# Retention attention by chunks of 128 tokens with carried sums, two head pairs at a time

## The chip, the cores and the metric

The kernel runs on one core of one Trainium2 chip. The metric is device time in microseconds: the median of a few runs of the whole launch.

## The reference

Eight batches of eight heads, 576 tokens and head size 64 go through a retention layer: scores are weighted by a power of gamma that depends on the distance, with no softmax. Its output, read as 4608 tokens of 512 features, goes through an MLP of width 2048 with a PReLU. Everything is fp32 (the MLP weights arrive as float64 bits).

```python
scores = (1.0 / np.sqrt(D)) * np.matmul(q, k.transpose(0, 1, 3, 2))
gamma = 1.0 - 2.0 ** (-5.0 - np.arange(H))
rel = pos[:, None] - pos[None, :]
Dmat = np.where(rel >= 0, gamma[:, None, None] ** rel[None], 0.0)
attn = np.matmul(scores * Dmat, v)                  # (B, H, S, D)
x = attn.transpose(0, 2, 1, 3).reshape(B * S, H * D)
h = x @ w_in
g = np.maximum(h, 0.0) + alpha * np.minimum(h, 0.0)
out = g @ w_out
```

## The kernel before

Heads are taken in pairs: 32 pairs (batch b, pair c), and two heads of 64 fill the 128 partitions. `load_pair` issues nine DMAs for a pair on SyncE's queue, two pairs ahead of use (three buffers). `transposes` turns Q and K to have the head dimension on partitions, ten 128-column TensorE transposes into PSUM tiles of the pool `ps_a`; ScalarE scales and copies Q out, VectorE copies K out. `scores` makes, for each of the five chunks of keys, the scores of all later queries (1600 columns for each head), in four groups that each fill a PSUM bank for each head; VectorE multiplies every piece by a table `decay` on its way to SBUF (line 245). `values` multiplies by V, 1600 columns for each head again, and ScalarE copies the result into x^T. The two heads of a pair use different halves of the TensorE array: different rows in the scores, different columns in the value products. A full fp32 matmul is two TensorE passes in the trace, each with a load of its stationary operand; a transpose is one.

The MLP runs in units of one block of 384 tokens and one chunk of 128 of the 2048 hidden features, 12 x 16 = 192 units: four products into `ph` (line 192), two VectorE operations for the PReLU (lines 196 and 198), three products into `po` (line 177). At the end of a block ScalarE copies `po` out and GpSimd's queue issues the stores (lines 183, 185).

The weights come in 32 pieces of 128 x 512 during the first two batches, four pieces for each pair. GpSimd issues the DMA of a piece (line 142); two GpSimd operations (149, 150), five on VectorE (151 to 161) and one more on GpSimd (163) round float64 bits to fp32. Two buffers hold raw pieces. The pieces alternate, four of `w_in` and four of `w_out`, so that each eight pieces make four more units of any block runnable.

The framework orders the instructions of each engine ahead of time from the order of the program, by its own estimates of readiness; at run time every engine executes its list in that order, and semaphores do the rest. Attention of batch b + 1 is written between MLP units of the batches up to b; batches 0 and 1 have no units written among them, but the framework may move units up. x^T is held in tiles of two batches, two buffers. `ps_a` has three buffers of one bank, `ph` two, `po` three.

Of the kernel before, what the change touches and what calls it, by code (L numbers as in the profile page):

```python
# [18 lines left out]
def kernel(  # L19
# [10 lines left out]
    nc = tc.nc  # L30
# [5 lines left out]
    NPAIR = H // 2              # head pairs in a batch; pair c fills rows c*128.. of x^T  # L36
    NCH = (S + P - 1) // P      # key chunks
    NFULL = S // P
    REM = S - NFULL * P
    msz = [min(P, S - P * i) for i in range(NCH)]  # L40
    NCC = DM // P
    NFC = DFF // P
    GB = 2                      # batches in one x^T tile
    TB = 384                    # tokens in an MLP block
    NTC = TB // P
    NKB = NTOK // TB
    SH = S // 2                 # queries in one pass of the value product
    WQ = 4                      # pieces in which the weights are loaded

    assert D == 64 and 2 * D == P and DM == H * D and NTOK == B * S  # L50
    assert (GB * S) % TB == 0 and B % GB == 0 and SH <= 512 and 0 < REM
    assert NPAIR == NCC and DM <= 512 and NFC % WQ == 0

    # Columns of chunk t in the transposed weights: queries P*t .. S.
    atoff = [sum(S - P * j for j in range(i)) for i in range(NCH)]
    ATW = sum(S - P * j for j in range(NCH))
    # Score groups, one PSUM bank each: (chunk, first query, last query, column in the bank)
    groups = [[(0, 0, 512, 0)],
              [(0, 512, S, 0), (1, P, S, S - 512)],
              [(2, 2 * P, S, 0), (3, 3 * P, S, S - 2 * P)],  # L60
              [(4, 4 * P, S, 0)]]
    assert S == 576 and NCH == 5
# [5 lines left out]
    nat = ctx.enter_context(tc.tile_pool(name="nat", bufs=3))  # L68
# [5 lines left out]

    pairs = [(b, c) for b in range(B) for c in range(NPAIR)]

    def load_pair(b, c):
        tiles = []
        for name, src in (("q", q), ("k", k), ("v", v)):
            t = nat.tile([P, NCH, 2, D], FP32, tag=f"nat_{name}", name=f"{name}n_{b}_{c}")  # L80
            for h2 in range(2):
                nc.sync.dma_start(
                    t[:, 0:NFULL, h2, :],
                    src[b, 2 * c + h2, 0:NFULL * P, :].rearrange("(j p) d -> p j d", p=P))
            nc.sync.dma_start(
                t[0:REM, NFULL, :, :],
                src[b, 2 * c:2 * c + 2, NFULL * P:S, :].rearrange("h p d -> p h d"))
            tiles.append(t)
        return tiles

    loaded = {0: load_pair(*pairs[0]), 1: load_pair(*pairs[1])}
# [4 lines left out]
    # decay[p, h, w] = gamma_h ** (w - p) for w >= p, otherwise 0.  The chunk t of  # L96
    # keys sees query s at w = s - P*t, so that one table serves all chunks.
    rel = const.tile([P, S], FP32, name="rel")
    nc.gpsimd.iota(rel, pattern=[[1, S]], base=0, channel_multiplier=-1,
                   allow_small_or_imprecise_dtypes=True)  # L100
    nc.gpsimd.affine_select(out=rel, in_=rel, compare_op=ALU.is_ge, fill=1.0e8,
                            base=0, pattern=[[1, S]], channel_multiplier=-1)
    decay = const.tile([P, H, S], FP32, name="decay")
    for h in range(H):
        nc.scalar.activation(decay[:, h, :], rel, ACTF.Exp,
                             scale=float(np.log1p(-(2.0 ** (-5.0 - h)))))
# [25 lines left out]
    # High words as fp32 patterns, which order as the doubles do: the largest whose  # L132
    # exponent fp32 has, and the smallest.
# [3 lines left out]
    def load_weights(n):  # L137
        for _ in range(min(n, len(pieces))):
# [9 lines left out]
            # Saturate above fp32's range, zero below it.  # L148
# [4 lines left out]
            # Sign and top exponent bit stay, the rest moves up by three: the double  # L153
            # cut to the 20 bits of mantissa in its high word.
# [4 lines left out]
            # The low word counts 2^-52 of the signed power of two.  # L159
# [8 lines left out]
    pend = []       # (block, chunk, activations) whose output products are still to come  # L168
# [42 lines left out]
    def transposes(qn, kn, b, c):  # L211
        qk = []
        for name, src in (("q", qn), ("k", kn)):
            dst = attn.tile([P, S], FP32, tag=f"{name}T", name=f"{name}T_{b}_{c}")
            for j0, j1 in ((0, 3), (3, NCH)):
                c0, c1 = j0 * P, min(j1 * P, S)
                pt = ps_a.tile([P, 512], FP32, tag="psa", name=f"pt{name}_{b}_{c}_{j0}")
                for j in range(j0, j1):
                    nc.tensor.transpose(  # L219
                        pt[:, j * P - c0:j * P - c0 + msz[j]],  # L220
                        src[0:msz[j], j, :, :].rearrange("p h d -> p (h d)"),
                        ident[0:msz[j], 0:msz[j]])
                if name == "q":
                    nc.scalar.mul(dst[:, c0:c1], pt[:, 0:c1 - c0], 1.0 / float(np.sqrt(D)))  # L224
                else:
                    nc.vector.tensor_copy(dst[:, c0:c1], pt[:, 0:c1 - c0])  # L226
            qk.append(dst)
        return qk

    def scores(qT, kT, b, c):  # L230
        at = [attn.tile([P, ATW], FP32, tag=f"at{h2}", name=f"at{h2}_{b}_{c}")
              for h2 in range(2)]
        for gi, grp in enumerate(groups):
            ps = [ps_a.tile([P, 512], FP32, tag="psa", name=f"ps{h2}_{b}_{c}_{gi}")
                  for h2 in range(2)]
            for t, s0, s1, co in grp:
                for h2 in range(2):
                    nc.tensor.matmul(ps[h2][0:msz[t], co:co + s1 - s0],  # L238
                                     kT[h2 * D:(h2 + 1) * D, P * t:P * t + msz[t]],
                                     qT[h2 * D:(h2 + 1) * D, s0:s1],  # L240
                                     start=True, stop=True)
            for h2 in range(2):
                for t, s0, s1, co in grp:
                    w0, w1 = s0 - P * t, s1 - P * t
                    nc.vector.tensor_tensor(  # L245
                        out=at[h2][0:msz[t], atoff[t] + w0:atoff[t] + w1],
                        in0=ps[h2][0:msz[t], co:co + s1 - s0],
                        in1=decay[0:msz[t], 2 * c + h2, w0:w1],
                        op=ALU.mult)
        return at  # L250

    def values(vn, at, b, c):
        grp, x0 = b // GB, (b % GB) * S
        for s0 in range(0, S, SH):
            s1 = s0 + SH
            po = ps_a.tile([P, 512], FP32, tag="psa", name=f"pv_{b}_{c}_{s0}")
            chunks = [t for t in range(NCH) if P * t < s1]
            for t in chunks:
                lo = max(s0, P * t)
                a0 = atoff[t] - P * t  # L260
                for h2 in range(2):
                    nc.tensor.matmul(po[h2 * D:(h2 + 1) * D, lo - s0:s1 - s0],  # L262
                                     vn[0:msz[t], t, h2, :],
                                     at[h2][0:msz[t], a0 + lo:a0 + s1],
                                     start=(t == chunks[0]), stop=(t == chunks[-1]))
            nc.scalar.copy(xT[grp][:, c, x0 + s0:x0 + s1], po[:, 0:SH])  # L266

    # Block kb of the MLP can start when the batch of its last token is done.
# [7 lines left out]
    WB = 2                                      # batches over which the weights arrive  # L276
    WPP = -(-len(pieces) // (WB * NPAIR))

    prev = None
    for i, (b, c) in enumerate(pairs):  # L280
        if c == 0 and b % GB == 0:
            xT[b // GB] = xpool.tile([P, NCC, GB * S], FP32, tag="xT", name=f"xT_{b // GB}")
        if i + 2 < len(pairs):
            loaded[i + 2] = load_pair(*pairs[i + 2])
        qn, kn, vn = loaded.pop(i)
        qT, kT = transposes(qn, kn, b, c)
        if prev is not None:
            values(*prev)
        if c == 0 and b > 0:
            enqueue(b - 1)  # L290
        share = -(-len(queue) // (NPAIR - c)) if b >= WB else 0
        pop_units(share // 2)
        at = scores(qT, kT, b, c)
        if b < WB:
            load_weights(WPP)
        pop_units(share - share // 2)
        prev = (vn, at, b, c)
    values(*prev)
    enqueue(B - 1)
    pop_units(len(queue))  # L300
    while pend:
# [31 lines left out]
```

## Time and profile before

| | us |
|---|---|
| median of 3 runs | 1415.12 (1414.74 to 1418.02) |
| span of the profiled execution | 1413.1 |
| TensorE busy with matmuls | 1343.5 |
| VectorE busy | 494.1 |
| GpSimd busy | 136.8 |
| ScalarE busy | 75.7 |

The span runs from the first to the last instruction of one execution that the hardware profiler recorded; that execution has no time of its own beside it, and the median of the runs lies 2.0 us above the span. Busy times of an engine are unions. TensorE's weight loads are counted apart (PEld) and overlap its matmuls (PE).

### The profile page before, as it was taken

How to read it: one execution, taken by the hardware profiler on the slowest of the kernel's cores; microseconds unless marked ns; L12 is line 12 of the kernel's file. 1: busy time of each engine (PE TensorE's matmuls, PEld its weight loads, DVE VectorE, ACT ScalarE, POOL GpSimd, SP SyncE). 2: the span in 40 equal slices, each digit the busy share in tenths (PEclk: the TensorE clock that was granted, in tenths of full speed). 3: DMA queues.
4: the chain of work that ended last, by engine and by line, in shares of the span. 5: the costliest groups of instructions: out<-in, count | busy, mean ns of one | idle time of the engine just before them, and what ended most of it. 6: DMA issues, size and time to landing. Idle time of an engine off the chain costs nothing.

```text
span 1413.1 us, 11632 instructions
## 1 busy us (share of the span) xinstructions
PE 1343.5 (95%) x4801; PEld 704.8 (50%) x4801; DVE 494.1 (35%) x993; ACT 75.7 (5%) x173; POOL 136.8 (10%) x173
## 2 busy tenths in 40 slices
PE   6878989999999999999999999999999999999997
PEld 3434444555545555554555555555555555555553
DVE  4677765323232333223223323332233232322221
ACT  2000000000000000000000100000000000000000
POOL 4544453000000000000000000000000000000000
PEclk9668789999999999999999999999999999999999
DMA  7434432010101111110110111101101100000000
GB/s 192 109 108 119 116 92 61 23 26 0 48 1 33 40 26 26 48 26 0 48 26 0 51 40 33 48 0 26 48 0 26 48 9 1 0 23 0 23 0 23
DMA packets 122773, 55.30 MB, mean 39 GB/s; under 512 B 116304, under 2 KB 116320, under 8 KB 122720
## 3 DMA queue, kind: packets, MB, share of 16 engines
q1 hardware_dynamic: 115200, 28.33, 9.0%
q0 software_dynamic: 7520, 26.23, 5.6%
q8 instruction: 38, 0.62, 0.2%
q14 instruction: 15, 0.12, 0.0%
HBM read 45.10 MB, written 9.44 MB: 39 GB/s over the span
## 4 chain that ended last, share of the span: by engine, by line
issue 44%; PE 40%; DMA 7%; POOL 5%; DVE 4%; SPq 0%; POOLq 0%; ACT 0%; ACTq 0%; DVEq 0%
PE ph L192 16%; PE po L177 16%; PE ps L238 4%; DMA raw<-in_moe_w_in_dram 3%; DMA raw<-in_moe_w_out_dram 3%; PE pv L262 3%; POOL wb L150 2%; DVE at L245 1%; POOL wa L149 1%; POOL w_in L163 1%; POOL w_out L163 1%; PE ptk L219 1%; POOL out_dram L185 1%; DVE wa L151 1%; PE ptq L219 1%
## 5 line engine op out<-in xcount | busy, mean ns | idle before, releaser
L192 PE MATMUL ph<-xT,w_in 128*128 128x384 f32 x1536 | 549.7, 495 | 0.0
L177 PE MATMUL po<-w_out,g 128*128 128x512 f32 x1152 | 536.7, 601 | 0.2 <-POOL wa L149 0.2
L192 PEld LDWEIGHTS ph<-xT,w_in 128*128 128x128 f32 x1536 | 285.1, 191 | 215.3 <-issue 73.3
L196 DVE TENSOR_SCALAR neg<-ph,alpha 128x384 f32<-128x384 f32 x192 | 118.5, 617 | 691.7 <-PE ph L192 691.7
L177 PEld LDWEIGHTS po<-w_out,g 128*128 128x128 f32 x1152 | 219.5, 192 | 233.4 <-issue 182.8
L238 PE MATMUL ps<-qT,kT 64*128 64x64 f32 (+5 forms) x768 | 167.5, 449 | 45.9 <-DVE at L245 43.2
L245 DVE TENSOR_TENSOR at<-ps,decay 128x192 f32<-128x192 f32 (+5 forms) x384 | 146.5, 426 | 88.9 <-PE ps L238 85.9
L238 PEld LDWEIGHTS ps<-qT,kT 64*128 64x128 f32 (+1 forms) x768 | 93.5, 189 | 154.5 <-DVE at L245 90.8
L185 POOL DMA_DIRECT2D out_dram<-osb x36 | 19.5, 542 | 1152.4 <-ACT osb L183 1152.4
L262 PE MATMUL pv<-at,vn 128*64 128x288 f32 (+4 forms) x1024 | 108.1, 359 | 3.3 <-DVE kT L226 2.8
L198 DVE SCALAR_TENSOR_TENSOR g<-ph,neg 128x384 f32<-128x384 f32 x192 | 106.9, 557 | 6.2
L262 PEld LDWEIGHTS pv<-at,vn 128*64 128x64 f32 (+1 forms) x1024 | 65.5, 144 | 45.9 <-issue 14.9
L224 ACT ACTIVATE qT<-ptq 128x384 f32<-128x384 f32 x64 | 23.3, 408 | 916.7 <-PE ptq L219 916.7
L226 DVE COPY kT<-ptk 128x384 f32<-128x384 f32 x64 | 29.0, 455 | 70.1 <-PE ptk L219 70.1
L151 DVE SCALAR_TENSOR_TENSOR wa<-wb,wa 128x512 f32<-128x512 f32 x32 | 36.1, 1128 | 44.6 <-POOL wb L150 44.5
L219 PE MATMUL ptk<-ident,kn 128*128 128x128 f32 (+1 forms) x160 | 34.2, 304 | 4.0 <-DMA kn<-in_k_dram 3.3
L183 ACT COPY osb<-po 128x512 f32<-128x512 f32 x36 | 21.1, 585 | 258.7 <-PE po L177 258.7
L150 POOL TENSOR_TENSOR wb<-wa 128x512 f32<-128x512 f32 x32 | 34.1, 1067 | 2.1
L266 ACT COPY xT<-pv 128x288 f32<-128x288 f32 x64 | 25.5, 399 | 153.4 <-PE pv L262 153.4
L219 PEld LDWEIGHTS ptq<-ident,qn 128*128 128x128 f32 (+1 forms) x160 | 21.6, 150 | 24.3 <-issue 19.2
L219 PE MATMUL ptq<-ident,qn 128*128 128x128 f32 (+1 forms) x160 | 29.2, 296 | 3.4 <-DVE at L245 3.4
L219 PEld LDWEIGHTS ptk<-ident,kn 128*128 128x128 f32 (+1 forms) x160 | 20.2, 150 | 21.4 <-issue 14.5
(23 smaller groups left out, 166.4 us busy)
## 6 DMA issues: line engine op xcount, KB each, us to landing
out_dram<-osb POOLq DMA_DIRECT2D x36, 256.0 KB, 2.4
qn<-in_q_dram SPq DMA_DIRECT2D x64, 128.0 KB, 2.5
kn<-in_k_dram SPq DMA_DIRECT2D x64, 128.0 KB, 2.8
raw<-in_moe_w_in_dram POOLq DMA_DIRECT2D x16, 512.0 KB, 4.3
vn<-in_v_dram SPq DMA_DIRECT2D x64, 128.0 KB, 2.6
raw<-in_moe_w_out_dram POOLq DMA_DIRECT2D x16, 512.0 KB, 3.7
qn<-in_q_dram SPq DMA_DIRECT2D x32, 32.0 KB, 2.6
kn<-in_k_dram SPq DMA_DIRECT2D x32, 32.0 KB, 2.5
```

The costliest lines, as they stand in the source:

```text
L150: nc.gpsimd.tensor_tensor(out=b, in0=a, in1=a, op=ALU.mult)
L151: nc.vector.scalar_tensor_tensor(out=a, in0=b, scalar=HI_MIN * HI_MIN, in1=a, op0=ALU.is_ge, op1=ALU.mult)
L177: nc.tensor.matmul(acc[kb][m], g[:, m * P:(m + 1) * P], w_out[fc // FCQ][:, fc % FCQ, :], start=(fc == 0), stop=(fc == NFC - 1))
L185: nc.gpsimd.dma_start(out[t0:t0 + P, :], osb)
L192: nc.tensor.matmul(ph, w_in[fc // FCQ][:, cc, f0:f0 + P], xT[grp][:, cc, t0:t0 + TB], start=(cc == 0), stop=(cc == NCC - 1))
L196: nc.vector.tensor_scalar(neg, ph, 0.0, alpha[:, fc:fc + 1], ALU.min, ALU.mult)
L198: nc.vector.scalar_tensor_tensor(out=g, in0=ph, scalar=0.0, in1=neg, op0=ALU.max, op1=ALU.add)
L219: nc.tensor.transpose(pt[:, j * P - c0:j * P - c0 + msz[j]], src[0:msz[j], j, :, :].rearrange("p h d -> p (h d)"), ident[0:msz[j], 0:msz[j]])
L226: nc.vector.tensor_copy(dst[:, c0:c1], pt[:, 0:c1 - c0])
L238: nc.tensor.matmul(ps[h2][0:msz[t], co:co + s1 - s0], kT[h2 * D:(h2 + 1) * D, P * t:P * t + msz[t]], qT[h2 * D:(h2 + 1) * D, s0:s1], start ...
L245: nc.vector.tensor_tensor(out=at[h2][0:msz[t], atoff[t] + w0:atoff[t] + w1], in0=ps[h2][0:msz[t], co:co + s1 - s0], in1=decay[0:msz[t], 2 ...
L262: nc.tensor.matmul(po[h2 * D:(h2 + 1) * D, lo - s0:s1 - s0], vn[0:msz[t], t, h2, :], at[h2][0:msz[t], a0 + lo:a0 + s1], start=(t == chunks ...
```

## The change

Attention is computed chunk by chunk. For a chunk j of 128 queries, the keys of the same chunk are handled by masked scores as before, but all earlier keys come in through a running sum of k^T v, a 64 x 64 matrix for each head, that is added up over the chunks. The decay is split into a factor on the query (`qtab`) and one on the key (`ktab`, `krem`), so that the scores need only a causal 0/1 mask. Sequences of 576 give four whole chunks and 64 tokens that are left; the rests of two head pairs are put side by side as one chunk of 128, with a block mask `maskr`.

Two pairs (a couple, four heads) are worked on together: 16 couples. Loads are 18 DMAs for each couple, buffers for two couples. GpSimd multiplies K by its factor in place, five operations for each couple. Each couple has 18 transposes, of which VectorE takes Q out with its factor and ScalarE takes K out. `scores` makes 18 products of 128 columns and masks them in six VectorE operations. `states`, new, makes 16 products of 64 columns and adds them up in eight VectorE operations of 64 partitions, into block-diagonal 128 x 128 matrices `sums` (two sets). `values` makes 18 products of 128 columns within the chunks and then eight full-width products of the sums with Q. The setup has some eighty small memsets and small tables in place of the 128 x 8 x 576 table. Values of a couple now come in the same step as its scores, with MLP units in three places, and the weights come in eight pieces for each couple. The MLP and the weight conversion are unchanged.

```diff
-    nat = ctx.enter_context(tc.tile_pool(name="nat", bufs=3))
+    nat = ctx.enter_context(tc.tile_pool(name="nat", bufs=2))
...
+    def load_couple(b, u):
+        tiles = []
+        for name, src in (("q", q), ("k", k), ("v", v)):
+            t = nat.tile([P, NJ, 4, D], FP32, tag=f"nat_{name}", name=f"{name}n_{b}_{u}")
+            r = nat.tile([P, 2, D], FP32, tag=f"rem_{name}", name=f"{name}r_{b}_{u}")
+            for j in range(NJ):
+                nc.sync.dma_start(
+                    t[:, j, :, :],
+                    src[b, 4 * u:4 * u + 4, j * C:(j + 1) * C, :].rearrange("h p d -> p h d"))
+            for i in range(2):
+                h = 4 * u + 2 * i
+                nc.sync.dma_start(
+                    r[i * REM:(i + 1) * REM, :, :],
+                    src[b, h:h + 2, NJ * C:S, :].rearrange("h p d -> p h d"))
+            tiles += [t, r]
+        return tiles
...
+    for j in range(NJ):
+        for h in range(H):
+            nc.gpsimd.memset(ktab[:, j, h:h + 1], float(np.exp(lng[h] * (MID - j * C))))
...
+            for j in range(NJ + 1):
+                nc.gpsimd.memset(qfac[rows, c, j:j + 1],
+                                 float(np.exp(lng[2 * c + h2] * (j * C - MID)) / np.sqrt(D)))
...
+    for i in range(2):
+        s_ = const.tile([P, NJ, 2, P], FP32, name=f"sums{i}")
+        nc.gpsimd.memset(s_, 0.0)
...
+    def transposes(n, b, u, tiles):
+        qn, qr, kn, kr, vn, vr = tiles
+        nc.gpsimd.tensor_tensor(
+            out=kr, in0=kr, in1=krem[:, u, :, None].to_broadcast([P, 2, D]), op=ALU.mult)
+        for j in range(NJ):
+            nc.gpsimd.tensor_tensor(
+                out=kn[:, j], in0=kn[:, j],
+                in1=ktab[:, j, 4 * u:4 * u + 4, None].to_broadcast([P, 4, D]), op=ALU.mult)
...
+        for i in range(2):
+            pt = ps_a.tile([P, NJ * C], FP32, tag="psa", name=f"ptq{i}_{n}")
+            for j in range(NJ):
+                nc.tensor.transpose(
+                    pt[:, j * C:(j + 1) * C],
+                    qn[:, j, 2 * i:2 * i + 2, :].rearrange("p h d -> p (h d)"), ident)
+            nc.vector.tensor_tensor(out=qT[i], in0=pt, in1=qtab[:, 2 * u + i, 0:NJ * C],
+                                    op=ALU.mult)
...
+            nc.scalar.copy(kT[i], pt)
+        return qT, kT, rT
+
+    def scores(n, qT, kT, rT):
+        at = []
+        for i in range(2):
+            ps = [ps_a.tile([P, NJ * C], FP32, tag="psa", name=f"ps{i}{h2}_{n}")
                   for h2 in range(2)]
+            for j in range(NJ):
                 for h2 in range(2):
+                    rows, cols = slice(h2 * D, (h2 + 1) * D), slice(j * C, (j + 1) * C)
+                    nc.tensor.matmul(ps[h2][:, cols], kT[i][rows, cols], qT[i][rows, cols],
+                                     start=True, stop=True)
             for h2 in range(2):
+                a = attn.tile([P, NJ, C], FP32, tag=f"at{i}{h2}", bufs=1, name=f"at{i}{h2}_{n}")
+                nc.vector.tensor_tensor(
+                    out=a, in0=ps[h2].rearrange("p (j w) -> p j w", w=C),
+                    in1=mask[:, None, :].to_broadcast([P, NJ, C]), op=ALU.mult)
+                at.append(a)
...
+    def states(n, tiles):
+        qn, qr, kn, kr, vn, vr = tiles
+        ps = ps_a.tile([P, NJ, 2, D], FP32, tag="psa", name=f"pu_{n}")
+        for j in range(NJ):
+            for i in range(2):
+                for h2 in range(2):
+                    nc.tensor.matmul(ps[h2 * D:(h2 + 1) * D, j, i, :], kn[:, j, 2 * i + h2, :],
+                                     vn[:, j, 2 * i + h2, :], start=(j == 0 and i == 0),
+                                     stop=(j == NJ - 1 and i == 1), skip_group_check=True)
+        sm = sums[n % 2]
+        for j in range(NJ):
+            for h2 in range(2):
+                hd = slice(h2 * D, (h2 + 1) * D)
+                if j == 0:
+                    nc.vector.tensor_copy(sm[hd, 0, :, hd], ps[hd, 0, :, :])
+                else:
+                    nc.vector.tensor_tensor(out=sm[hd, j, :, hd], in0=ps[hd, j, :, :],
+                                            in1=sm[hd, j - 1, :, hd], op=ALU.add)
+
+    def values(n, b, u, tiles, qT, rT, at):
...
+        for i in range(2):
+            for j in range(NJ):
                 for h2 in range(2):
+                    nc.tensor.matmul(pv[i][h2 * D:(h2 + 1) * D, j * C:(j + 1) * C],
+                                     vn[:, j, 2 * i + h2, :], at[2 * i + h2][:, j, :],
+                                     start=(j == 0), stop=False, skip_group_check=True)
...
+        for i in range(2):
+            for j in range(1, NJ):
+                nc.tensor.matmul(pv[i][:, j * C:(j + 1) * C], sm[:, j - 1, i, :],
+                                 qT[i][:, j * C:(j + 1) * C],
+                                 start=False, stop=(j == NJ - 1), skip_group_check=True)
+            nc.scalar.copy(xT[grp][:, 2 * u + i, x0:x0 + NJ * C], pv[i])
...
+    for n, (b, u) in enumerate(couples):
...
+        share = -(-len(queue) // (NC2 - u)) if b >= WB else 0
+        qT, kT, rT = transposes(n, b, u, tiles)
+        pop_units(share // 3)
+        at = scores(n, qT, kT, rT)
+        states(n, tiles)
         if b < WB:
+            load_weights(WPC)
+        pop_units(share // 3)
+        values(n, b, u, tiles, qT, rT, at)
+        pop_units(share - 2 * (share // 3))
+        if u == NC2 - 1:
+            enqueue(b)
```

## Rows read from the trace of the kernel before

**Rows 1.** The page's slices: TensorE's busy share in 40 equal slices, in tenths.

```profile
PE   6878989999999999999999999999999999999997
```

**Rows 2.** Line 163, last step of a weight piece: count, duration min/median/max, first and last start.

```profile
L163 POOL TENSOR_TENSOR w_out<-wa,wb x16: 1250/1260/1649, 46.0 to 233.4; 128x512 f32<-128x512 f32 x16
```

**Rows 3.** Windows, 0 to 234.7 us: busy time and count by engine, granted clock, DMA.

```profile
0.00:234.70 234.70, 194.34 (x753) 101.12 (x755) 159.91 (x313) 20.27 (x46) 117.30 (x137) 0.82 0.45 118
```

**Rows 4.** Chain of waits, 95 to 130 us: start, length, what.

```profile
99.05 3.55 DMA raw<-in_moe_w_out_dram
...
102.76 0.66 POOL wa L149
...
103.49 1.03 POOL wb L150
104.53 1.18 POOL w_out L163
105.70 3.74 DMA raw<-in_moe_w_out_dram
```

**Rows 5.** Windows, 234.7 to 1405.2 us, of lines 192, 177, 238 and 262 in turn.

```profile
234.70:1405.20 1170.50, 507.89 (x1438) 265.72 (x1438) 1.00 0.09 23
...
234.70:1405.20 1170.50, 495.40 (x1086) 206.34 (x1086) 1.00 0.09 23
...
234.70:1405.20 1170.50, 104.83 (x552) 60.09 (x552) 1.00 0.09 23
...
234.70:1405.20 1170.50, 74.03 (x756) 45.36 (x752) 1.00 0.09 23
```

**Rows 6.** Timeline of TensorE, 1303 to 1316 us: start, length, instructions.

```profile
1304.45 2.74 PE L192 MATMUL ph<-xT,w_in 128*128 128x384 f32 x8
...
1309.61 2.74 PE L192 MATMUL ph<-xT,w_in 128*128 128x384 f32 x8
```

**Rows 7.** Chain of waits, 670 to 790 us: one head pair among MLP units.

```profile
677.00 0.65 PE ph L192 x2
677.96 3.06 PE pv L262 x32
...
701.19 1.11 PE ps L238 x4
...
706.28 0.84 PE ph L192 x2
707.38 2.13 PE ph L192 x6
...
729.63 3.07 PE pv L262 x32
```

**Rows 8.** Timeline of TensorE, 1399 to 1406 us: the last products.

```profile
1399.82 5.31 PE L177 MATMUL po<-w_out,g 128*128 128x512 f32 x12
```

**Rows 9.** Timeline, 675 to 683 us: the transposes of Q and their loads.

```profile
675.72 0.80 PE L219 MATMUL ptq<-ident,qn 128*128 128x128 f32 x5
675.72 0.36 PEld L219 LDWEIGHTS ptq<-ident,qn 128*128 128x128 f32 x3 [0.29 <-issue]
```

**Rows 10.** Groups by line and shape, VectorE, line 245: busy us, mean ns, idle before.

```profile
L245 DVE TENSOR_TENSOR at<-ps,decay 128x512 f32<-128x512 f32 x64 | 41.9, 685 | 61.9 <-PE ps L238 61.9
...
L245 DVE TENSOR_TENSOR at<-ps,decay 128x192 f32<-128x192 f32 x64 | 22.1, 346 | 0.0
...
L245 DVE TENSOR_TENSOR at<-ps,decay 128x64 f32<-128x64 f32 x64 | 13.9, 218 | 13.2 <-PE ps L238 13.2
```

**Rows 11.** Timeline, 0 to 40 us: two small memsets of GpSimd.

```profile
0.31 0.10 POOL L317 MEMSET const-bfloat16-1.0<- 128x1 bf16 x1
0.35 0.10 POOL L317 MEMSET const-uint8-127<- 128x1 uint8 x1
```

**Rows 12.** Groups by line and shape: TensorE's weight loads of lines 238 and 262.

```profile
L238 PEld LDWEIGHTS ps<-qT,kT 64*128 64x128 f32 x640 | 80.2, 198 | 114.2 <-DVE at L245 60.1 <-issue 34.5 <-PE po L177 3.0
L262 PEld LDWEIGHTS pv<-at,vn 128*64 128x64 f32 x896 | 59.3, 145 | 37.0 <-issue 6.0 <-DVE kT L226 3.0 <-DVE wa L160 0.8
```

More of the change, by code (lines that the diff above doesn't have):

```diff
@@ L36 @@
     NPAIR = H // 2
[L37 to L40, printed above, removed]
+    NC2 = NPAIR // 2
+    C = P
+    NJ = S // C
+    REM = S - NJ * C
+    MID = S // 2
     NCC = DM // P
@@ L46 @@
     NKB = NTOK // TB
-    SH = S // 2
     WQ = 4
     assert D == 64 and 2 * D == P and DM == H * D and NTOK == B * S
[L51 to L62, printed above, removed]
+    assert (GB * S) % TB == 0 and B % GB == 0 and 2 * REM == P and NJ == 4
+    assert NPAIR == NCC and DM <= 512 and NFC % WQ == 0 and NC2 == 2
     const = ctx.enter_context(tc.tile_pool(name="const", bufs=1))
@@ L73 @@
     ps_o = ctx.enter_context(tc.tile_pool(name="ps_o", bufs=NTC, space=bass.MemoryType.PSUM))
-    pairs = [(b, c) for b in range(B) for c in range(NPAIR)]
-    def load_pair(b, c):
+    couples = [(b, u) for b in range(B) for u in range(NC2)]
+    def load_couple(b, u):
         tiles = []
         for name, src in (("q", q), ("k", k), ("v", v)):
-            t = nat.tile([P, NCH, 2, D], FP32, tag=f"nat_{name}", name=f"{name}n_{b}_{c}")
-            for h2 in range(2):
+            t = nat.tile([P, NJ, 4, D], FP32, tag=f"nat_{name}", name=f"{name}n_{b}_{u}")
+            r = nat.tile([P, 2, D], FP32, tag=f"rem_{name}", name=f"{name}r_{b}_{u}")
+            for j in range(NJ):
@@ L89, in load_pair @@
+            tiles += [t, r]
         return tiles
-    loaded = {0: load_pair(*pairs[0]), 1: load_pair(*pairs[1])}
+    loaded = {0: load_couple(*couples[0]), 1: load_couple(*couples[1])}
     ident = const.tile([P, P], FP32, name="ident")
     make_identity(nc, ident)
-    rel = const.tile([P, S], FP32, name="rel")
-    nc.gpsimd.iota(rel, pattern=[[1, S]], base=0, channel_multiplier=-1,
+    lng = [float(np.log1p(-(2.0 ** (-5.0 - h)))) for h in range(H)]
+    wrow = const.tile([P, C], FP32, name="wrow")
@@ L100 @@
+    nc.gpsimd.iota(wrow, pattern=[[1, C]], base=0, channel_multiplier=0,
                    allow_small_or_imprecise_dtypes=True)
-    nc.gpsimd.affine_select(out=rel, in_=rel, compare_op=ALU.is_ge, fill=1.0e8,
-                            base=0, pattern=[[1, S]], channel_multiplier=-1)
-    decay = const.tile([P, H, S], FP32, name="decay")
-    for h in range(H):
-        nc.scalar.activation(decay[:, h, :], rel, ACTF.Exp,
-                             scale=float(np.log1p(-(2.0 ** (-5.0 - h)))))
+    prow = const.tile([P, 1], FP32, name="prow")
@@ new lines @@
+    nc.gpsimd.iota(prow, pattern=[[1, 1]], base=0, channel_multiplier=1,
+                   allow_small_or_imprecise_dtypes=True)
+    mask = const.tile([P, C], FP32, name="mask")
+    nc.gpsimd.memset(mask, 1.0)
+    nc.gpsimd.affine_select(out=mask, in_=mask, compare_op=ALU.is_ge, fill=0.0,
+                            base=0, pattern=[[1, C]], channel_multiplier=-1)
+    maskr = const.tile([P, C], FP32, name="maskr")
+    nc.vector.tensor_copy(maskr, mask)
+    nc.vector.memset(maskr[0:REM, REM:C], 0.0)
@@ new lines @@
+    for u in range(NC2):
+        for i in range(2):
+            rows = slice(i * REM, (i + 1) * REM)
+            for h2 in range(2):
+                h = 4 * u + 2 * i + h2
+                nc.vector.tensor_scalar(
+                    krem[rows, u, h2:h2 + 1], kpow[rows, h:h + 1],
+                    float(np.exp(lng[h] * (MID - NJ * C + i * REM))), None, ALU.mult)
+    qtab = const.tile([P, NPAIR, NJ * C + REM], FP32, name="qtab")
+    lgq = const.tile([P, NPAIR], FP32, name="lgq")
+    qpow = const.tile([P, NPAIR, C], FP32, name="qpow")
@@ L208, in pop_units @@
             mlp_unit(*queue.pop(0))
[L211 to L228, printed above, removed]
@@ new lines, in scores @@
+                a = attn.tile([P, NJ, C], FP32, tag=f"at{i}{h2}", bufs=1, name=f"at{i}{h2}_{n}")
+                nc.vector.tensor_tensor(
+                    out=a, in0=ps[h2].rearrange("p (j w) -> p j w", w=C),
+                    in1=mask[:, None, :].to_broadcast([P, NJ, C]), op=ALU.mult)
+                at.append(a)
+        for h2 in range(2):
+            rows = slice(h2 * D, (h2 + 1) * D)
+            ps = ps_a.tile([P, C], FP32, tag="psa", name=f"psr{h2}_{n}")
+            nc.tensor.matmul(ps, rT[rows, 1, :], rT[rows, 0, :], start=True, stop=True)
+            a = attn.tile([P, C], FP32, tag=f"atr{h2}", bufs=1, name=f"atr{h2}_{n}")
+            nc.vector.tensor_tensor(out=a, in0=ps, in1=maskr, op=ALU.mult)
+            at.append(a)
@@ L276 @@
     WB = 2
[L277 to L281, printed above, removed]
+    WPC = -(-len(pieces) // (WB * NC2))
+    for n, (b, u) in enumerate(couples):
+        if u == 0 and b % GB == 0:
             xT[b // GB] = xpool.tile([P, NCC, GB * S], FP32, tag="xT", name=f"xT_{b // GB}")
[L283 to L293, printed above, removed]
-        if b < WB:
[L295 to L299, printed above, removed]
+        if n + 2 < len(couples):
+            loaded[n + 2] = load_couple(*couples[n + 2])
+        tiles = loaded.pop(n)
+        share = -(-len(queue) // (NC2 - u)) if b >= WB else 0
[3 more added lines that the diff above has]
+        states(n, tiles)
+        if b < WB:
+            load_weights(WPC)
[4 more added lines that the diff above has]
+            enqueue(b)
     pop_units(len(queue))
```

86 lines of the change are left out of this document (51 added, 35 removed).

## Prediction

> **What bounds the kernel now.** I read the page's slices first. TensorE shows 6 to 9 tenths in the first seven slices and 9 from there to the end [rows 1]; cut where the last weight piece is written, at 234.7 us [rows 2], the profile falls into two stages with different limits.
>
> *Stage one, 0 to 234.7 us.* TensorE is busy for 194 us of it, at a granted clock of 0.82, a mean over its two levels [rows 3]; no engine is full. The chain of waits tells what sets the length: over its middle it holds nothing but the weight conversion, one piece after the other, 3.6 us of DMA, then three GpSimd operations of 0.66, 1.03 and 1.18 us, and the next DMA starts 6.65 us after the last (7.0 and 7.1 for the two that follow) [rows 4]. 32 pieces at about 7.1 us, behind a start of some 7, are the 234 us. The first MLP block needs the last quarter of the weights, so at the end of this stage only 98 of 1536 first-product passes and 66 of 1152 second-product ones are done (an fp32 matmul is two passes), while attention is about 8.7 head pairs along: 552 of 768 score passes, 23 pairs of 24 passes, and 756 of 1024 value passes, 23.6 pairs, are left [rows 5].
>
> *Stage two, 234.7 to 1405.1 us.* Here TensorE sets the pace. Eight passes of 384 columns and six of 512 make an MLP unit, and two units start 5.16 us apart [rows 6]: 0.322 us a first pass, 0.430 a second. Between two pairs' value products there are 51.67 us, with eight units in them [rows 7]; 51.67 - 8 x 5.155 = 10.43 us is what a head pair costs. Test: 1438 x 0.322 + 1086 x 0.430 = 930 us of MLP, and 23.3 x 10.43 = 243 us of attention, together 1173 against 1170.5 measured. The last 8 us to 1413.1 are the copies and stores behind the last product [rows 8].
>
> So the time is stage one + 930 + (pairs left) x 10.43 + 8. The profiled execution's span is 1413.1 us; the median of the runs, 1415.1, lies 2.0 above, and I add that at the end.
>
> **The change, part by part.** Two pairs (a couple) now go together, 16 couples. Counting columns from the code, a couple had 2 x (1600 score + 1600 value) columns in each half of the array, and now has 1152 score, 512 state, 1152 value and 896 full-width carry columns; transposes stay at about 18 for 20. What 20.86 us becomes I work out stage by stage.
>
> *Transposes.* Five took 0.80 us of which the last one's own tail is 0.27, so they start some 0.13 us apart [rows 9]: 18 x 0.13 = 2.3 us. They fill five PSUM tiles and the pool has three buffers: the fourth tile waits for the first one's eviction, 0.69 us on VectorE for 512 columns [rows 10]. I add 0.5 for two such waits: 2.8 us.
>
> *Scores.* In the old pair, the first group, 512 columns for each head, took 1.11 us, and the stage from 701.19 to 707.38, less 0.64 us of two MLP passes moved into it, 5.5 us [rows 7]. It is paced by VectorE emptying three buffers. The new one has the same first group, then four evictions of 0.69 us, and two of 128 columns at 0.28 (between the 0.22 and 0.35 of 64 and 192 columns [rows 10]): 1.11 + 2.74 + 0.56 = 4.4 us for two pairs.
>
> *States.* 16 products of 64 columns, two passes each, two side by side: 16 steps at 64/128 of a 128-column pass. The old value products give 3.07 us for 2 x 1600 columns, two side by side [rows 7], 0.96 ns a column: 16 x 64 x 0.96 = 1.0 us. The eight running sums behind them are VectorE work of about 0.28 each, 2.2 us; MLP units stand between them and the carry that reads them, so I cost them at nothing; without that cover 2.2 us a couple.
>
> *Values.* 36 passes of 128 columns, two side by side, 18 x 128 x 0.96 = 2.2 us; the carry has no partner: 12 x 128 + 4 x 64 columns at 0.96 = 1.7 us. Together 3.9.
>
> Sum 2.8 + 4.4 + 1.0 + 3.9 = 12.1, and 0.5 for changes between these forms (the old pair's parts, 1.6 + 3.07 + 5.5, leave 0.25 of its 10.43 over): **12.6 us a couple against 20.9**. If the scheduler fills every PSUM wait with MLP work, the scores cost 18 x 128 x 0.96 = 2.2 and the transposes 2.3, some 10; if the sums and the waits all lie open, 15.
>
> *Queues.* K's decay moves to GpSimd: four multiplies of 256 elements and one of 128 a couple, at 1.03 us for 512 [rows 4], 2.3 us. In stage two GpSimd has only the stores; I cost it at nothing, covered by loads that come a couple ahead; behind a store it would be late by the copies and issues of a block's end, about 3 us. In stage one it stands in the queue that sets the length. For most of each weight DMA's 3.55 us GpSimd waits [rows 4], where a couple's five fit, so most of it should hide: 3 us in all for the first five couples, 12 if none does. The new tables need about 80 small memsets ahead of the first weight DMA; small ones were 0.10 us long and started 0.035 apart [rows 11], so 3 to 8 us, less 1.3 us for the wide iota and select that go, and two wide memsets of sums: I take +5. VectorE gets lighter, an estimated 7.4 us a couple for 11.9 at prices between those of [rows 10], but in stage one it waits for GpSimd, not the other way; nothing for it. Q's scaling moves from ScalarE to VectorE and K's copy the other way, both under MLP work. Loads: 18 a couple as before, the same bytes, off the path. Weights in groups of eight instead of four: same pieces, same chain.
>
> Stage one then ends at 234.7 + 5 + 3 = 242.7, rounded down to 241 for a little less waiting on VectorE; bounds 215 (pieces at 6.6 us) to 260. As before I take some 0.7 of a couple beyond the first four as done by then: 11.3 left. **241 + 930 + 11.3 x 12.6 + 8 = 1321, with the 2.0 us 1323.** What the first four couples save buys nothing, since the weights end that stage.
>
> **The rivals.** *Weight loads come into the open* (the other side). The change cuts the columns of a pass to 128 and 64, but issues 138 passes a couple for 132, each with its own load of the stationary operand. A load of 128 columns lasts 0.198 us, one of 64 columns 0.145 [rows 12], as long as the new passes or longer; under 288 to 512 columns they were hidden. If each stood ahead of its step: scores 18 x 0.198, states and values 34 x 0.145, carry 16 x 0.198 = 11.7 us more, 24.3 us a couple, 1456 us. It decides from 20.7 us a couple on, 70% of the loads in the open. Against it: the transposes' passes of 128 columns start 0.13 apart, with three loads of 128 columns in 0.36 us among them [rows 9], which leaves no room for load and pass in turn. The Trainium skill, in "TensorE: Matmul & The Clock Gate", section Part 3: Packing small matmuls, says that a load overlaps running matmuls only where the row group differs. By that rule the state, value and carry loads stay in the open, 8.1 us more, and the time would be 1415, as before. The trace's transposes, all in one row group, go against it.
>
> *Stage one grows.* GpSimd's order is fixed, and a K multiply that waits for its load, or stands behind the DMA wait rather than in it, delays every later piece; at 8.5 us a piece the stage ends 45 us later: 1368. For it: the chain there has no slack [rows 4]. Against: GpSimd was busy for only half of the stage [rows 3].
>
> *Stage one takes in more.* Lighter couples run ahead while MLP waits for weights. Two x^T buffers allow batches 0 to 3, eight couples; eight left at 12.6, and pieces at 6.6 us: 225 + 930 + 101 + 8 + 2 = 1266. For it: TensorE has 40 us idle there and runs at 0.82. Against: the old kernel had the same room and ran 0.7 of a pair ahead.
>
> **How the numbers follow.** My forecast 0.58; more taken in 0.17; stage one grows 0.16; loads in the open 0.09, of which a third lands within 0.3% (about what a measurement of this kernel can tell from no change). The range runs from the one neighbour to the other, 1262 to 1372, which leaves out the loads and little else. Faster 0.91, same 0.03, slower 0.06.
>
> **What would show it.** Right: TensorE at 9 tenths from about 240 us; a gap of some 12 to 13 us beside whole MLP units in a couple; passes of 128 columns starting 0.11 apart, two side by side; evictions, not loads, ending TensorE's waits in the scores; the last weight piece written at 235 to 250. Wrong: steps of 0.25 us or more; GpSimd multiplies standing between DMA landing and conversion; TensorE waiting on GpSimd's K in stage two, or couples 5 to 8 done before the weights are.

## The result and the profile after

The changed kernel takes 1277.99 us (median of 4 runs, 1276.65 to 1281.41) against 1414.93 us on the same chip: a ratio of 0.903, 95% interval 0.901 to 0.905. The forecast was 1323 with a range of 1262 to 1372: direction and range held, the gain came out 45 us larger than forecast. The profiled execution's span is 1276.2 us, so 1.8 us lie around it, as 2.0 did before.

The page of the changed kernel, its slices in tenths: the same two stages as in [rows 1]. GpSimd is busy for 153 of the first 250 us, where it was for 117 of 235 [rows 3].

```profile
PE   5788887899999999999999999999999999999997
```

The last weight piece's end is the end of stage one, as in [rows 2]. The last step of the conversion is now line 211 (count, duration min/median/max, first and last start):

```profile
L211 POOL TENSOR_TENSOR w_out<-wa,wb x16: 1256/1267/1647, 55.5 to 249.1; 128x512 f32<-128x512 f32 x16
```

Stage one ends at 250.4 us, 16 later than before (249.1 is where that last step starts). What is left at that point answers to [rows 5]. Windows of the changed kernel for lines 240 (first product), 225 (second product) and 304 (scores) in turn; the columns are length, TensorE busy, weight loads, clock, DMA:

```profile
250.40:1268.40 1018.00, 488.58 (x1400) 261.27 (x1400) 1.00 0.08 22
...
250.40:1268.40 1018.00, 484.55 (x1062) 201.70 (x1062) 1.00 0.08 22
...
250.40:1268.40 1018.00, 29.81 (x320) 25.98 (x320) 1.00 0.08 22
```

Stage one got further than before: 136 and 90 MLP passes behind it (98 and 66 before), and six couples' scores (320 of 512 passes left, ten couples) where 8.7 pairs had been done. MLP still to come is 1400 x 0.322 + 1062 x 0.430 = 907 us. TensorE's last product ends at 1267.9, so 1267.9 - 250.4 - 907.4 = 110 us are the ten couples: **11.0 us each**, forecast 12.6, against 20.9 for two pairs. The chain of waits over one couple, which answers to [rows 7]:

```profile
574.67 1.90 PE pv L349 x32
576.57 0.22 PE pvr L353 x4
576.78 1.53 PE pv L358 x12
578.32 0.39 PE pvr L363 x4
...
609.70 0.87 PE ptq L274 x8
...
610.79 0.65 PE ph L240 x2
611.44 0.87 PE ptk L290 x8
...
637.44 1.14 PE ps L304 x16
638.59 0.68 DVE at L308
...
640.47 0.84 PE ph L240 x2
641.31 0.42 PE psr L315 x2
641.73 0.84 PE ph L240 x2
642.57 1.08 PE pu L327 x32
...
668.33 1.90 PE pv L349 x32
```

Transposes take 609.70 to 612.31 less two MLP passes, 1.96 us; scores 637.44 to 642.57 less two such pairs (0.84 each), 3.45; states 1.08; values 1.90 + 0.22 + 1.53 + 0.39 = 4.04. With the four MLP passes in the scores taken off at an undisturbed 0.322, as the prediction did, the scores are 3.84. The two value stages of the chain start 93.66 us apart with 16 units in between; less 16 x 5.155 that is 11.2 us for a couple, a little over the 11.0, because the transposes of a seventh couple were done in stage one. Only one wait on an eviction (a copy out of PSUM) is left on the chain of a couple, 0.68 us; behind the others stand MLP passes. 32 passes of 128 columns in 1.90 us are 16 steps of 0.119, two heads side by side.

One account will serve for all runs below. Span less 990 us of MLP (192 x 5.155), less attention at its stage-two price, less 8 us at the end, is what stage one *loses*: 1413.1 - 990 - 32 x 10.43 - 8 = 81 us before, 1276.2 - 990 - 16 x 11.0 - 8 = 102 us after (99 at 11.2 a couple). So attention became 158 us cheaper, counted over all 32 pairs, and stage one lost 21 us more; the difference is the 137 us of the result.

### The profile page after: what moved, and what is told of

The parts are those of the page before. It is cut to its first block, busy times and chain, and to the rows that moved or that the text cites. A ratio compares the mean times of both kernels' runs of the same rounds, so it can differ in the third digit from the quotient of the medians.

```text
span 1276.2 us, 11815 instructions
## 1 busy us (share of the span) xinstructions
PE 1204.7 (94%) x4897; PEld 676.0 (53%) x4897; DVE 448.2 (35%) x852; ACT 63.7 (5%) x129; POOL 195.0 (15%) x337
## 4 chain that ended last, share of the span: by engine, by line
PE 56%; issue 27%; DVE 5%; POOL 5%; DMA 5%; SPq 1%; POOLq 0%
PE po L225 25%; PE ph L240 25%; DMA raw<-in_moe_w_in_dram 3%; PE ps L304 2%; DMA raw<-in_moe_w_out_dram 2%; DVE wa L209 1%; POOL wb L198 1%; DVE wb L205 1%; PE pv L349 1%; POOL w_in L211 1%; POOL wa L197 1%; POOL w_out L211 1%; PE pv L358 1%; SPq L75 1%; PE pu L327 1%
## 5 line engine op out<-in xcount | busy, mean ns | idle before, releaser
L265 POOL TENSOR_TENSOR kn<-kn,ktab 128x256 f32<-128x256 f32 x64 | 43.7, 698 | 171.1 <-DMA kn<-in_k_dram 170.9
L304 PE MATMUL ps<-qT,kT 64*128 64x128 f32 x512 | 52.3, 296 | 11.4 <-DVE at L308 7.7
L304 PEld LDWEIGHTS ps<-qT,kT 64*128 64x128 f32 x512 | 45.2, 198 | 28.3 <-DVE at L308 12.0
L308 DVE TENSOR_TENSOR at<-ps,mask 128x512 f32<-128x512 f32 x64 | 41.9, 684 | 32.8 <-PE ps L304 32.8
L349 PEld LDWEIGHTS pv<-at,vn 128*64 128x64 f32 x512 | 30.6, 147 | 9.8 <-issue 8.1
L349 PE MATMUL pv<-at,vn 128*64 128x128 f32 x512 | 34.3, 289 | 0.0
L358 PE MATMUL pv<-qT,sums 128*128 128x128 f32 x192 | 27.2, 286 | 2.6 <-DVE sums L337 2.6
L337 DVE TENSOR_TENSOR sums<-pu,sums 64x128 f32<-64x128 f32 x96 | 27.7, 289 | 3.0
L197 POOL TENSOR_SCALAR wa<-raw 128x512 f32<-128x512 f32 x32 | 22.4, 699 | 39.9 <-DMA raw<-in_moe_w_in_dram 26.3
L205 DVE SCALAR_TENSOR_TENSOR wb<-wa,wb 128x512 int32<-128x512 int32 x32 | 27.7, 864 | 0.5
```

What stands on the lines that cost most here:

```text
L197: nc.gpsimd.tensor_scalar(a, hi, HI_MAX, -HI_MAX, ALU.min, ALU.max)
L205: nc.vector.scalar_tensor_tensor(out=bi, in0=ai, scalar=-0x40000000, in1=bi, op0=ALU.bitwise_and, op1=ALU.bitwise_or)
L265: nc.gpsimd.tensor_tensor(out=kn[:, j], in0=kn[:, j], in1=ktab[:, j, 4 * u:4 * u + 4, None].to_broadcast([P, 4, D]), op=ALU.mult)
L304: nc.tensor.matmul(ps[h2][:, cols], kT[i][rows, cols], qT[i][rows, cols], start=True, stop=True)
L308: nc.vector.tensor_tensor(out=a, in0=ps[h2].rearrange("p (j w) -> p j w", w=C), in1=mask[:, None, :].to_broadcast([P, NJ, C]), op=ALU.mult)
L349: nc.tensor.matmul(pv[i][h2 * D:(h2 + 1) * D, j * C:(j + 1) * C], vn[:, j, 2 * i + h2, :], at[2 * i + h2][:, j, :], start=(j == 0), stop=F ...
```

## The experiments

Two questions. What did the couples of stage one bring: nothing, as the prediction had it, or their full saving? And where do the 21 us come from? Each ratio is taken against the kernel before on the run's own chip (1412 to 1415 us there). The gains in microseconds are differences from the 1278.0 of the changed kernel, measured apart from them; since the kernel before differs by up to 3 us between the sets of runs, they are good to some 3 us.

**Attention of the first four couples left out.** Their scores, states and values are skipped, and x^T is filled with a copy of K^T.

```diff
-        at = scores(n, qT, kT, rT)
-        states(n, tiles)
+        if n >= 4:
+            at = scores(n, qT, kT, rT)
+            states(n, tiles)
...
+        else:
+            for i in range(2):
+                nc.scalar.copy(xT[b // GB][:, 2 * u + i, x0:x0 + NJ * C], kT[i])
```

> The changed kernel without scores, states and values of the first four couples (batches 0 and 1); their part of x^T is copied from K^T instead, so the output differs there. The rows give 3.45 + 1.08 + 4.04 = 8.6 us of TensorE a couple for these steps. Theory A (whatever TensorE time the weight stage leaves is used by the next ready work, so a saving in the first couples counts in full): 4 x 8.6 = 34 us faster, some 1244 us, 1236 to 1254. Theory B (as predicted: the weights end that stage, and what the first four couples save buys nothing): within 5 us of 1278. If the last weight piece is written much earlier than 250 us, VectorE's freed time did it, and the two have to be told apart by the work done up to that point.

Measured: 1254.6 us, ratio 0.888 (0.885 to 0.890): 23 us faster. Theory B is out, and theory A holds in part only. The last piece and the scores left (line 304):

```profile
L211 POOL TENSOR_TENSOR w_out<-wa,wb x16: 1257/1324/1650, 53.7 to 241.5; 128x512 f32<-128x512 f32 x16
...
242.80:1246.90 1004.10, 25.01 (x272) 21.75 (x272) 1.00 0.08 21
```

Stage one ends 7.6 us earlier; the expectation named VectorE's freed time as the likely cause of such a shift, and no run separates it. 272 score passes left are 8.5 couples, and 288 value passes left are nine. So of the couples that still count, 3.5 by scores and three by values were done in stage one, in place of two: 1 to 1.5 x 11.0, some 11 to 16 us pulled ahead. The MLP left is the same but for four passes. The two make 19 to 24; the spans differ by 21. What TensorE got back and spent on later work is thus under half of the 34 us, and clearly not nothing.

**K's multiplies left out.** `transposes` begins without its five GpSimd operations, so K has no decay factor.

```diff
-        nc.gpsimd.tensor_tensor(
-            out=kr, in0=kr, in1=krem[:, u, :, None].to_broadcast([P, 2, D]), op=ALU.mult)
-        for j in range(NJ):
-            nc.gpsimd.tensor_tensor(
-                out=kn[:, j], in0=kn[:, j], ...
```

> The changed kernel without the five multiplies of K by its decay factor on GpSimd for each couple (K goes in as loaded, so the decay is wrong). They are 64 operations of 0.70 and 16 of 0.48 us, 3.3 us a couple, 24 of the 64 and more in the weight stage. As predicted (most of them hide in GpSimd's wait for the weight DMA, 3 us in all): 1273 to 1278. Rival (they stand in the queue that converts the weights and make up the larger part of the 21 us that this stage lost more than in the kernel before): 10 to 20 us faster, 1258 to 1268, with the last piece written at 230 to 240.

Measured: 1262.7 us, ratio 0.894 (0.892 to 0.896): 15 us faster, the rival. The last piece of this run:

```profile
L211 POOL TENSOR_TENSOR w_out<-wa,wb x16: 1254/1266/1652, 53.7 to 234.4; 128x512 f32<-128x512 f32 x16
```

Stage one ends at 235.7, 14.7 us earlier, with ten couples' states and values, the scores of 9.25 couples and the same MLP left: nearly the whole gain is length of that stage. The timeline of the changed kernel's GpSimd shows why a multiply doesn't hide. Start, length, operation:

```profile
43.78 0.61 POOL L190 DMA_DIRECT2D raw<-in_moe_w_out_dram  x1
44.41 3.01 POOL L265 TENSOR_TENSOR kn<-kn,ktab 128x256 f32<-128x256 f32 x4
47.39 0.84 POOL L262 TENSOR_TENSOR kr<-kr,krem 128x128 f32<-128x128 f32 x1
48.21 0.63 POOL L197 TENSOR_SCALAR wa<-raw 128x512 f32<-128x512 f32 x1
```

Here they do stand behind a weight DMA, as I had hoped, but five of them are 3.85 us, as long as the wait. And in this list GpSimd often works on a piece while the next one is on its way, so there is less wait to hide in than [rows 4] showed: 40 us in all at the first step of a piece, against 87 in the kernel before (first row, there line 149). The columns are busy us and mean ns, then the idle time before and what ended it.

```profile
L149 POOL TENSOR_SCALAR wa<-raw 128x512 f32<-128x512 f32 x32 | 22.0, 688 | 86.6 <-DMA raw<-in_moe_w_in_dram 46.6 <-DMA raw<-in_moe_w_out_dram 39.6
...
L197 POOL TENSOR_SCALAR wa<-raw 128x512 f32<-128x512 f32 x32 | 22.4, 699 | 39.9 <-DMA raw<-in_moe_w_in_dram 26.3 <-DMA raw<-in_moe_w_out_dram 13.4
L265 POOL TENSOR_TENSOR kn<-kn,ktab 128x256 f32<-128x256 f32 x32 | 24.4, 785 | 4.5 <-DMA kn<-in_k_dram 4.4
```

The last row is the K multiplies up to 250 us: 32 of them, for eight couples already, at 0.785 us where I had 0.52.

**Weight conversion cut to one operation**, in both kernels; the weights are then not the rounded float64.

```diff
-            nc.gpsimd.tensor_scalar(a, hi, HI_MAX, -HI_MAX, ALU.min, ALU.max)
...
-            nc.gpsimd.tensor_tensor(out=dst, in0=a, in1=b, op=ALU.add)
+            nc.gpsimd.tensor_scalar(dst, hi, HI_MAX, -HI_MAX, ALU.min, ALU.max)
```

> The kernel before, with one GpSimd operation for each weight piece in place of four on GpSimd and five on VectorE (so the weights are not the rounded float64). By sums from rows: 192 x 5.155 = 990 us of MLP, 32 x 10.43 = 334 of attention and 8 at the end leave 81 us that the weight stage costs. If the conversion causes these, some 65 of them go: 1340 to 1360 us. Rival (they come from the start, the loads of Q, K and V and the clock): 1395 or more.

Measured: 1349.2 us, ratio 0.955 (0.952 to 0.957): 64 us of the old kernel's 81 go, as expected.

> The changed kernel, with the same cut of the weight conversion. 990 + 16 x 11.0 + 8 leaves 102 us that the weight stage costs here. If the conversion causes these: 1185 to 1210 us, and the distance to the kernel before with the same cut is 145 to 160 us (16 couples at 9.8 us) in place of 137. Rival (setup, K on GpSimd and loads cost a good part of the 102 by themselves): 1215 to 1240, a distance of 110 to 130.

Measured: 1224.1 us, ratio 0.866 (0.864 to 0.868): the rival's range, 125 us from the old kernel with the same cut. Of its 102 us 49 stay (span 1222.7), where the old kernel keeps 17. Without the conversion the new kernel thus loses 32 us more than the old one, not 21: something in its couples or its setup costs time in stage one by itself. Its chain of waits names K's multiplies and DMA landings in the first 100 us, and its TensorE waits for K itself: line 247 is the multiply here, 272 the transpose of K.

```profile
10.44 3.33 POOL kn L247 x4
...
PE ptk L272 <- POOL kn L247: 18.0, 8, 3.4
```

How much of the 49 us they are was only read from the chain; this cut was not run without them.

**Parts of a couple left out.** First the eight products of the carried sums with Q in `values`.

> The changed kernel without the eight full-width products of the carried sums with Q in each couple (the sums are still made; what earlier chunks contribute is left out). In the second stage these products take 1.53 + 0.39 = 1.9 us of a couple's 11.0. If TensorE's own columns set the price of a couple: 10 x 1.9 = 19 us in the second stage and about a third of 6 x 1.9 in the weight stage, 20 to 28 us faster, 1250 to 1258. Rival (VectorE's emptying of PSUM sets it): 1270 or more.

Measured: 1251.5 us, ratio 0.886 (0.885 to 0.888), 26.5 us faster. TensorE ends at 1239.1; stage one at 247.8 with 288 score passes, nine couples, and the same MLP left: (1239.1 - 247.8 - 907.4) / 9 = 9.3 us a couple. 1.7 us fewer for 1.9 us of products: TensorE's columns set the price of a couple. Of the spans' 29 us that is 15; the other 14 came in stage one, which ended 2.6 us earlier and got one couple further, where the expectation had 4. So here about all that the first six couples saved (6 x 1.9 = 11.5) came back.

Then VectorE's eight additions a couple, with the products on sums that stay zero.

> The changed kernel without VectorE's eight operations a couple that add up the sums (they stay zero; their products are still made). They take 8 x 0.289 = 2.3 us of VectorE a couple, 37 us in all. As predicted (MLP units cover them) they cost nothing in the second stage; in the weight stage VectorE now stands in the chain, and six couples there give at most 14 us: 1264 to 1277. Rival (VectorE paces the couples throughout): 1240 to 1250.

Measured: 1263.9 us, ratio 0.895 (0.894 to 0.897), 14 us faster, at the very edge of the range. Stage one ends at 238.8, 11.6 earlier, and (1256.1 - 238.8 - 907.4) / 10 = 11.0 us a couple: nothing in stage two, all in stage one. The 14 and the 15 of K's multiplies are more than the 21 us together, so they can't simply be added, and no run leaves out both.

**K's factor on another engine**, the whole computation. On ScalarE:

```diff
...
+        for j in range(NJ):
+            for h4 in range(4):
+                nc.scalar.mul(kn[:, j, h4, :], kn[:, j, h4, :],
+                              ktab[:, j, 4 * u + h4:4 * u + h4 + 1])
```

> The changed kernel with K's decay factor put on by ScalarE: 18 operations of 64 columns a couple in place of five on GpSimd, the whole computation. ScalarE is busy for 5% of the span. If the 15 us that K's multiplies cost come from standing in GpSimd's queue: 1259 to 1267. Rival (ScalarE's 18 operations, some 4 us, delay its copies of K^T and x^T in the weight stage by as much as they free): 1272 to 1285.

Measured: 1261.6 us, ratio 0.894 (0.892 to 0.895): as good as without the multiplies. ScalarE was nearly idle.

On VectorE, `nc.vector` for `nc.gpsimd`:

> The changed kernel with K's five multiplies a couple on VectorE, the whole computation. At 0.685 us for 512 columns they are 4 x 0.35 + 0.2 = 1.6 us a couple, about half of GpSimd's 3.3. If only GpSimd's queue is tight in the weight stage: 1260 to 1267, as on ScalarE. If VectorE stands in that chain as well (a fifth of it by the chain of waits): half of the gain is lost, 1267 to 1274.

Measured: 1266.7 us, ratio 0.898 (0.896 to 0.899): where the two expectations meet; on VectorE some 5 of the 16 us are lost again. Stage one ends at 231.1 there, 4.5 us earlier than with ScalarE, but the values of one couple less are done in it.

**More buffers for the weights**, with K's factor on ScalarE.

```diff
-            raw = wraw.tile([P, FQ, 2], INT32, tag="raw", name=f"raw_{at}")
+            raw = wraw.tile([P, FQ, 2], INT32, tag="raw", bufs=3, name=f"raw_{at}")
```

> K's factor on ScalarE, and three buffers for the raw weights in place of two, the whole computation. In the weight stage GpSimd still waits some 50 us for the weight DMA to land; a third buffer lets it be issued a piece earlier. If that wait sets the stage's length: 30 us or more off it, of which a half to two thirds is time: 1235 to 1248. Rival (the order of GpSimd's list and VectorE's operations set it, and the DMA is only late because of them): 1255 to 1265.

Measured: **1242.3 us, ratio 0.878 (0.877 to 0.880)**, the fastest version of the whole computation. Stage one ends near 202 us, 34 earlier than with two raw buffers, and 19 us of that are time, as first expected.

A third buffer for `wa` too:

> The same with three buffers for the first working tile of a weight piece as well, the whole computation, so that a piece's first operation need not wait for the last one of the piece two before. If the working tile is what holds the next piece back, this one is faster than with three raw buffers alone by 10 us or more; otherwise the two agree within 5 us.

Measured: 1277.8 us, ratio 0.904 (0.902 to 0.905): 35 us *slower* than with three raw buffers alone, which neither expectation had. Windows of 60 to 120 and 120 to 180 us (columns as in [rows 3]), first with three raw buffers, then with both:

```profile
60.00:120.00 60.00, 50.65 (x342) 34.03 (x342) 53.22 (x102) 15.50 (x52) 36.60 (x40) 0.94 0.58 154
120.00:180.00 60.00, 52.34 (x228) 28.52 (x227) 46.86 (x82) 5.27 (x19) 39.92 (x43) 0.94 0.37 109
```

```profile
60.00:120.00 60.00, 40.63 (x288) 33.37 (x289) 58.52 (x91) 17.93 (x61) 41.93 (x43) 0.67 0.58 155
120.00:180.00 60.00, 46.76 (x148) 25.10 (x147) 58.35 (x77) 2.02 (x5) 43.30 (x45) 0.90 0.36 109
```

VectorE is full in the second (third busy figure, 58 of 60 us), and TensorE gets 10 and 6 us less, at a clock of 0.67 in the first window. Below that, in the same order: first-product passes done by 200 us (line 240) and the first step of the PReLU (line 244; count, duration min/median/max, first and last start).

```profile
0.00:200.00 200.00, 50.38 (x138) 25.37 (x138) 0.91 0.57 150
...
L244 DVE TENSOR_SCALAR neg<-ph,alpha x192: 601/617/619, 67.2 to 1227.5; 128x384 f32<-128x384 f32 x192
```

```profile
0.00:200.00 200.00, 31.09 (x80) 15.63 (x80) 0.80 0.56 146
...
L244 DVE TENSOR_SCALAR neg<-ph,alpha x192: 604/618/619, 126.8 to 1264.5; 128x384 f32<-128x384 f32 x192
```

The weights are ready at the same time in both (last step at 200.6 and 198.2). 138 against 80 first-product passes, and 84 against 48 second ones, are 58 x 0.322 + 36 x 0.430 = 34 us: nearly the whole difference. So the weights don't set what TensorE gets. What differs is VectorE, in two ways. Its list has a new order: the first PReLU starts at 126.8 us, 60 later than with three raw buffers, though the first MLP products start near 57 us in both runs. And its conversion steps got longer: from 60 to 120 us the five of a piece take 4.45 us in place of 3.48. What each of the two is worth was not separated.

At last, on top of that, the conversion's square on ScalarE:

> The same again with the square in the weight conversion on ScalarE in place of GpSimd (it is only compared with a threshold), the whole computation. It takes 1.03 us of some 3.5 us of GpSimd's work a piece out, 33 us in all. If GpSimd's list sets the weight stage: 10 to 20 us faster than without. Rival (VectorE, with 3.6 us a piece and the evictions, sets it): within 5 us.

Measured: 1262.7 us, ratio 0.893 (0.891 to 0.895). 15 us faster than the run before it, as expected from GpSimd's list, and still 20 behind three raw buffers alone. Stage one ends at 174.5 here, 27 us before that of the fastest version, but with 72 first-product passes done in place of 138; the first PReLU starts at 121.8, as late as in the run before it.

## Why the prediction was right, and where it missed

**The mechanism was right** for stage two; the account of stage one was not. The time is stage one, then MLP at its old price, then couples at a new one, and the couple's price comes from TensorE's columns: the run without the carry shows it.

**The price of a couple was mis-sized**, 12.6 for 11.0. States and values came as worked out (1.08 for 1.0, 4.04 for 3.9). Transposes (1.96 for 2.8) and scores (3.45 to 3.84 for 4.4) were priced with waits for a PSUM buffer standing open; in the trace MLP passes stand behind all but one of them. The transposes come out below even the lower bound of their term, because they start 0.109 us apart and not the 0.13 read from five of them. Over 11.3 couples the 1.6 are 18 us.

**The step that failed** is "What the first four couples save buys nothing, since the weights end that stage", and with it "11.3 left". Leaving out attention there bought 23 us. Stage one has a length, but it isn't filled: TensorE time that an early couple gives back goes to the next ready work, in that run and in the one without the carry to later couples. How large a part comes back is open: under half of 34 us in the one, about all of 11.5 in the other. In the changed kernel 23 us of MLP and 1.3 couples more than forecast were done inside stage one; that the MLP part has the same cause is inferred, for no run shows it alone. Couples five and six done before the weights was one of the prediction's own signs of being wrong. The rival "stage one takes in more" described the direction, by ten couples left, not its eight.

**GpSimd's price was too low.** I took 3 us for K's multiplies, "most of it should hide", and 12 if none does. They cost 15: they run in stage one for eight couples, not five, take 0.785 us in place of 0.52, and find less wait than the old order showed. So stage one ended at 250.4, not 241. The "stage one grows" rival had the right mechanism, its 45 us was three times too much. The setup's 5 us came as worked out: the first weight DMA is issued at 7.87 us, in place of 3.08. The additions of the sums, costed at nothing behind MLP units, were that in stage two, but 14 us in stage one, nearly all of it length of that stage; "nothing for it" on VectorE there was wrong.

The terms: stage one 9 us later than forecast, 907 for 930 us of MLP, 110 for 142 us of couples, the end as forecast: 9 - 23 - 32 = -46 us, up to rounding the distance of 1276 from the 1321 of the sum. Two errors of one sign (the couples, the work inside stage one) were partly covered by one of the other (its length).

**Weight loads stayed hidden.** The value products issue 32 passes in 1.90 us with loads of 0.147 us each, two heads side by side, and the loads run in the same stretch:

```profile
668.26 1.73 PEld L349 LDWEIGHTS pv<-at,vn 128*64 128x64 f32 x32 [0.76 <-issue]
...
670.38 1.42 PEld L358 LDWEIGHTS pv<-qT,sums 128*128 128x128 f32 x12 [0.17 <-issue]
```

If each load stood ahead of its step, 16 steps would take 16 x (0.119 + 0.147) = 4.3 us. The carry's passes have no partner and use the whole array: 12 in 1.53 us, 0.128 each, with loads of 0.192. The Trainium skill's rule in "TensorE: Matmul & The Clock Gate", section Part 3: Packing small matmuls, that loads overlap running matmuls only in another row group, does not agree with this trace: both kinds of passes use all rows.

## What to carry to other kernels

Where a stage is paced by a queue off the bottleneck engine, its length is only half of the account: ask how much work of the bottleneck engine gets done in it, since part of the time saved there is spent on the next ready work. Before moving an operation onto a queue "with idle time", check that this queue isn't the one in the chain; ScalarE, idle for 95%, took the same work at no cost that shows (1261.6 us, against 1262.7 without the work). And a buffer more can change the order of another engine's list: a third raw buffer gave 19 us, one more buffer for the next tile took 35 back.

## What the runs showed of the hardware

A slowly fed TensorE pays twice. In the changed kernel it stood still for 3.23 us before 184.46, waiting for a weight piece, and the next six passes of 512 columns took 4.54 us at a mean granted clock of 0.61 (much of it at the lower of the two levels, 1.2 GHz); six such passes at 190.13, at a clock of 1.00, took 2.74.

```profile
184.46 4.54 PE L225 MATMUL po<-w_out,g 128*128 128x512 f32 x6 [3.23 <-POOL w_out L211]
...
190.13 2.74 PE L225 MATMUL po<-w_out,g 128*128 128x512 f32 x6
```

A GpSimd multiply took 0.40 us at least for 128 elements and 0.60 for 256, against 1.03 for 512 (the last without a broadcast operand): small operations there are dearer than their elements.

VectorE's conversion steps and GpSimd's operations took longer where they ran side by side. The rows are one of these steps with three raw buffers, then with three `wa` buffers as well:

```profile
L205 DVE SCALAR_TENSOR_TENSOR wb<-wa,wb x32: 676/679/686, 22.6 to 197.2; 128x512 int32<-128x512 int32 x32
...
L205 DVE SCALAR_TENSOR_TENSOR wb<-wa,wb x32: 673/950/2046, 22.9 to 195.0; 128x512 int32<-128x512 int32 x32
```

In the first run none of the 32 lies beside a computing GpSimd operation. In the second 28 do, and take 1.13 us on average; the other four take 0.683. VectorE's masking of the scores out of PSUM (line 308) keeps its time there, 0.674 to 0.693 us, beside such operations or not. In the changed kernel the K multiply of 256 elements took 0.605 to 0.616 us in stage two, and up to 1.15 in stage one, 0.785 on average.
